# Multi-query attention with a GELU branch: some of the exp tiles on VectorE as integer bit patterns, four-head groups and a list scheduler

## The chip, the cores and the metric

The kernel runs on one core of one Trainium2 chip. The metric is the device time of the program in microseconds. It is taken several times per kernel, and each execution comes with the mean clock that TensorE was granted (1.0 is full speed). An execution is called slow when it lies over 1.5% above the fastest of the same kernel. Only fast ones are compared, unless the text says otherwise. Engines: PE is TensorE, PEld its weight loads, DVE VectorE, ACT ScalarE, POOL GpSimd.

## The reference

```python
B, S, D, H, F = 1, 2048, 512, 32, 1792          # Dh = D // H = 16
xn = _layernorm(x)
q = (xn @ wq).reshape(B, S, H, Dh).transpose(0, 2, 1, 3)
k, v = xn @ wk, xn @ wv                          # one K and one V for all 32 heads
scores = jnp.einsum("bhqd,bkd->bhqk", q, k) * (Dh ** -0.5)
o = jnp.einsum("bhqk,bkd->bhqd", softmax(scores), v)
A = o.transpose(0, 2, 1, 3).reshape(B, S, H * Dh) @ wo
Bb = gelu(xn @ w1 + b1, approximate=True) @ w2 + b2
return x + A + Bb                                # bf16 in and out
```

Attention needs 32 x 2048 x 2048 exponentials. In tiles of 128 keys by 512 queries these are 2048 tiles.

## The kernel before

It processes queries in four blocks of 512, heads in groups of three (and one of two), and keys in 16 tiles of 128. One step makes three score tiles in three PSUM banks (row-tiled matmuls of 17 rows: 16 of the head and one that subtracts an upper bound of the scores), one wide exp on ScalarE, and three column-tiled PV matmuls into a fourth bank. Two sets of three banks alternate. The GELU branch, the projections of Q and the outputs are woven in, two matmuls a step. Where a step has none of these, the same number of idle "fill" matmuls is issued, meant to keep TensorE's clock up.

```python
GROUPS = [list(range(h, min(h + 3, H))) for h in range(0, H, 3)]
...
def exp(s):
    act(lambda e: e.activation(E[:, s % NEB, 0:n * TBW], bank(3 * x, n), ACT.Exp, scale=0.25), ...)

def pv(s):
    for j, h in enumerate(GROUPS[g]):
        mm(pO[32 * j:32 * j + 32, :], V1[:, kt, :], E[:, s % NEB, j * TBW:(j + 1) * TBW],
           kt == 0, kt == NT - 1, r=["V1", ("E", s % NEB)], w=[B(6)], tp=(0, 32 * j))
...
for s in range(NS):
    exp(s)
    if s + 2 < NS:
        fill(s, n_fill)          # idle matmuls into the bank that comes next
        scores(s + 2)
    pv(s)
    ...                          # group ends, tanh, gates, up to two woven-in matmuls
```

Of the kernel before, what the change touches and what calls it, by code (L numbers as in the profile page):

```python
# [7 lines left out]
ALU = mybir.AluOpType  # L8
AX = mybir.AxisListType

P = 128
GELU_C = 0.044715
GELU_K = 0.7978845608028654


class _Op:
    __slots__ = ("eng", "fn", "deps", "stream", "amt", "need", "ticket", "waits", "clock")


class Prog:  # L20



# [5 lines left out]
    def __init__(self, nc):  # L29
        self.nc = nc  # L30
        self.ops = []
        self.writer = {}
        self.readers = {}

    def add(self, eng, fn, r=(), w=(), dma=None):
        op = _Op()
        op.eng, op.fn = eng, fn
        op.stream = dma or eng
        op.amt = 16 if dma else 1
        op.need = bool(dma)  # L40
        op.ticket = None
        deps = {}

        def dep(o, raw):
            if o is None:
                return
            if o.stream == eng and (eng == "pe" or not raw):
                return
            deps[id(o)] = o

        for k in r:
            dep(self.writer.get(k), True)
        for k in w:
            dep(self.writer.get(k), False)
            for o in self.readers.get(k, ()):
                dep(o, False)
        op.deps = list(deps.values())
        for o in op.deps:
            o.need = True
        for k in w:  # L60
            self.writer[k] = op
            self.readers[k] = []
        for k in r:
            self.readers.setdefault(k, []).append(op)
        self.ops.append(op)
        return op

    def emit(self):
# [41 lines left out]
        return {s: t for s, t in count.items()}  # L110


def bass_parallel_sum__grouped_kv_mqa__dense_activation_gelu__prompt_kernel(
# [24 lines left out]
    GROUPS = [list(range(h, min(h + 3, H))) for h in range(0, H, 3)]  # L138
    NGR = len(GROUPS)
    NEB = 4  # L140
# [3 lines left out]
    with ExitStack() as es:  # L144
# [4 lines left out]
        xn = sb([P, 8, D], bf, "xn")  # L149
# [3 lines left out]
        wq_s = sb([P, DT, D], bf, "wq_s")  # L153
        wkp = sb([P, DT, 4, 32], bf, "wkp")
        wqp = sb([P, DT, H, 32], bf, "wqp")
        wop = sb([96, NGR, D], bf, "wop")
# [4 lines left out]
        ident = sb([P, P], bf, "ident")  # L161
        ones = sb([P, P], bf, "ones")
# [5 lines left out]
        selL = sb([64, 2], f32, "selL")  # L168
        rT = sb([P, 4, 2], f32, "rT")
        rX = sb([P, 4, 64], f32, "rX")  # L170
# [17 lines left out]
        V1 = sb([P, NT, 32], bf, "V1")  # L188
        QT = sb([P, 2, 8, TBW], bf, "QT")
        sqq = sb([P, 2, TBW], bf, "sqq")  # L190
        mT = sb([32, 2, TBW], bf, "mT")
        E = sb([P, NEB, 3 * TBW], bf, "E")
        Of = sb([96, 2, TBW], f32, "Of")
        den = sb([96, 2, 16], f32, "den")
        rbc = sb([96, 2, TBW], f32, "rbc")
        rd_dram = nc.dram_tensor("rden_rows", [NTB * NGR, 3 * TBW], f32).ap()
        oT = sb([96, 2, NGR, TBW], bf, "oT")
        hb = sb([P, FT, TBW], bf, "hb")
        ub = sb([P, FT, TBW], bf, "ub")
        xpy = sb([P, 4, D], f32, "xpy")  # L200
        outb = sb([P, 4, D], bf, "outb")
# [13 lines left out]
        def dve(fn, r=(), w=()):  # L215
            return add("dve", fn, r, w)

        def act(fn, r=(), w=()):
            return add("act", fn, r, w)

        def pool(fn, r=(), w=()):
            return add("pool", fn, r, w)

        def mm(o, l, rh, start, stop, r=(), w=(), tp=None, skip=False):
# [5 lines left out]
            return add("pe", lambda e: e.matmul(o, l, rh, start=start, stop=stop, **kw), r, w)  # L230

        def dma(eng, o, i, stream, r=(), w=()):
            return add(eng, lambda e: e.dma_start(o, i), r, w, dma=stream)

# [7 lines left out]
        dma("sp", wq_s[:], A_wq.rearrange("(k p) n -> p k n", p=P), "d_wq", w=["wq_s"])  # L242
# [3 lines left out]

# [15 lines left out]
        pool(lambda e: e.memset(V1[:, :, Dh:32], 0.0), w=["V1"])  # L262
        pool(lambda e: e.memset(V1[:, :, Dh:Dh + 1], 1.0), r=["V1"], w=["V1"])
# [14 lines left out]

# [3 lines left out]
        def ln_batch(b):  # L282
# [3 lines left out]
            for ti in range(t0, t0 + 4):  # L286
                dve(lambda e, ti=ti: e.bn_aggr(mv[:, ti, :], stats[:, ti, :]), r=[("st", ti)], w=[("mv", b)])
            sl = slice(t0, t0 + 4)
            dve(lambda e: e.tensor_scalar(ve_b[:, sl], mv[:, sl, 1], 1e-5, None, ALU.add), r=[("mv", b)], w=[("ve", b)])
            act(lambda e: e.activation(std_b[:, sl], ve_b[:, sl], ACT.Sqrt), r=[("ve", b)], w=[("std", b)])  # L290
            dve(lambda e: e.tensor_copy(m_b[:, sl], mv[:, sl, 0]), r=[("mv", b)], w=[("mb", b)])
            if b < 3:
                ln_stats(t0 + 4)
            dve(lambda e: e.reciprocal(rstd[:, sl], std_b[:, sl]), r=[("std", b)], w=[("rstd", b)])
            dve(lambda e: e.scalar_tensor_tensor(nmr[:, sl], m_b[:, sl], -1.0, rstd[:, sl], ALU.mult, ALU.mult),
                r=[("mb", b), ("rstd", b)], w=[("nmr", b)])
            on_act = [t0, t0 + 2] if b == 3 else []
            for ti in range(t0, t0 + 4):
                if ti in on_act:
                    act(lambda e, ti=ti: e.activation(xn[:, ti % 8, :], x_sb[:, ti, :], ACT.Identity,  # L300
                                                      bias=nmr[:, ti:ti + 1], scale=rstd[:, ti:ti + 1]),
                        r=[("x", ti), ("rstd", b), ("nmr", b)], w=[("xn", ti % 8)])
                else:
                    pool(lambda e, ti=ti: e.tensor_scalar(xn[:, ti % 8, :], x_sb[:, ti, :], rstd[:, ti:ti + 1],  # L304
                                                          nmr[:, ti:ti + 1], ALU.mult, ALU.add),
                         r=[("x", ti), ("rstd", b), ("nmr", b)], w=[("xn", ti % 8)])
# [5 lines left out]
        def x_T(b):  # L312
            order = [4 * b, 4 * b + 1, 4 * b + 2, 4 * b + 3]
            for ti in order:
                bk = ti % 2
                pT = bank(bk)[:, 0:256].bitcast(bf)
                for d in range(DT):
                    add("pe", lambda e, ti=ti, d=d, pT=pT: e.transpose(  # L318
                        pT[:, d * P:(d + 1) * P], xn[:, ti % 8, d * P:(d + 1) * P], ident[:]),
                        r=[("xn", ti % 8), "ident"], w=[B(bk)])  # L320
# [4 lines left out]
        def k_proj(b):  # L325
# [5 lines left out]
            act(lambda e: e.activation(KT[:, c], bank(bk), ACT.Identity, bias=krow[:, 0:1]),  # L331
# [10 lines left out]
        def q_proj(tb, hq, bk):  # L342
            for d in range(DT):
                mm(bank(bk), wqp[:, d, 4 * hq:4 * hq + 4, :].rearrange("p a n -> p (a n)"),
                   xnT[:, d, tb * TBW:(tb + 1) * TBW], d == 0, d == DT - 1, r=["wqp", ("xnT", tb)], w=[B(bk)])
                yield

        def q_evac(tb, hq, bk):
            pq, i = tb % 2, hq % 2
            dve(lambda e: e.tensor_copy(QT[:, pq, hq, :], bank(bk)), w=[B(bk), ("QT", pq, hq)])  # L350
            dve(lambda e: e.tensor_tensor(sqq[:, i, :], QT[:, pq, hq, :], QT[:, pq, hq, :], ALU.mult),
                r=[("QT", pq, hq)], w=[("sqq", i)])

        def q_first(hq, bk):
            for _ in q_proj(0, hq, bk):
                pass
            q_evac(0, hq, bk)

        def q_first_m(hq, bk):
            mm(bank(bk), selrR[:].rearrange("p a n -> p (a n)"), sqq[:, hq % 2, :], False, True,  # L360
               r=["selrR", ("sqq", hq % 2)], w=[B(bk)], skip=True)
            dve(lambda e: e.tensor_scalar(QT[:, 0, hq, :].bitcast(i16), bank(bk).bitcast(i32), isc[:, 0:1], ibi[:, 0:1],
                                          ALU.mult, ALU.add),
                r=["isc", "ibi"], w=[B(bk), ("QT", 0, hq)])

        def v_tiles(ts, first=False):
            for ti in ts:
                for d in range(DT):
                    mm(pO[:, ti * Dh:(ti + 1) * Dh], xnT[:, d, ti * P:(ti + 1) * P], wv_s[:, d, :], d == 0, d == DT - 1,
                       r=["wv_s", ("xnT", ti // 4)], w=[B(6)])  # L370
# [13 lines left out]
            r=["wq_s", "wqp"], w=["wqp"])  # L384
# [13 lines left out]
        dve(lambda e: e.tensor_reduce(R2[:], kmax[:], AX.X, ALU.max), r=["kmax"], w=["R2"])  # L398
# [3 lines left out]
        dve(lambda e: e.tensor_copy(V1[:, :, 0:Dh], pO[:, 0:NT * Dh].rearrange("p (t n) -> p t n", n=Dh)),  # L402
            r=["V1"], w=[B(6), "V1"])
        warm(4, 3)


        steps = [(tb, g, kt) for tb in range(NTB) for g in range(NGR) for kt in range(NT)]
        NS = len(steps)

        def scores(s):  # L410
            tb, g, kt = steps[s]
            x = s % 2
            for j, h in enumerate(GROUPS[g]):
                q0 = 32 * (h % 4)
                mm(bank(3 * x + j), KT[q0:q0 + 17, kt * P:(kt + 1) * P], QT[q0:q0 + 17, tb % 2, h // 4, :],
                   True, True, r=[("KT", kt // 4), ("QT", tb % 2, h // 4)], w=[B(3 * x + i) for i in range(3)],
                   tp=(q0, 0))

        def exp(s):
            tb, g, kt = steps[s]  # L420
            x = s % 2
            n = len(GROUPS[g])
            act(lambda e: e.activation(E[:, s % NEB, 0:n * TBW], bank(3 * x, n), ACT.Exp, scale=0.25),  # L423
                w=[B(3 * x + i) for i in range(3)] + [("E", s % NEB)])

        def pv(s):
            tb, g, kt = steps[s]
            for j, h in enumerate(GROUPS[g]):
                mm(pO[32 * j:32 * j + 32, :], V1[:, kt, :], E[:, s % NEB, j * TBW:(j + 1) * TBW],
                   kt == 0, kt == NT - 1, r=["V1", ("E", s % NEB)], w=[B(6)], tp=(0, 32 * j))  # L430

        def o_evac(tb, g):
            n = len(GROUPS[g])
            i = (tb * NGR + g) % 2
            dve(lambda e: e.tensor_copy(Of[0:32 * n, i, :], pO[0:32 * n, :]), w=[B(6), ("Of", i)])  # L435
            row = Of[16:17, i, :]
            dma("sp", den[0:32 * n, i, :], bass.AP(row.tensor, row.offset, [[32 * row.ap[0][0], n], [1, TBW]]),
                f"d_den{i}", r=[("Of", i)], w=[("den", i)])

        def o_recip(tb, g):  # L440
            n = len(GROUPS[g])
            i = (tb * NGR + g) % 2
            rows = rd_dram[tb * NGR + g:tb * NGR + g + 1, 0:n * TBW]
            dve(lambda e: e.reciprocal(den[0:32 * n, i, :], den[0:32 * n, i, :]), r=[("den", i)], w=[("den", i)])  # L444
            dma("sp", rows, den[0:32 * n, i, :], f"d_rd{i}", r=[("den", i)], w=[("rd", i)])
            for j in range(n):
# [268 lines left out]
```

## Time and profile before

| | before |
|---|---|
| timed, median of 3 (lowest to highest) | 1032.86 us (1024.54 to 1051.49) |
| span of the profiled execution | 1027.0 us |
| ScalarE busy | 966.7 us, 94% |
| TensorE busy | 904.4 us, 88% (idle fill matmuls included) |
| VectorE busy | 303.0 us, 30% |

Of the three, 1051.49 is slow by the rule above. The page's first part gives busy time by engine, and its chain of waits tells which engine the end hung on. The prediction shows both. In the stretch between the first and the last exp, the view of windows gives, after the stretch and its length, the busy time and the number of instructions of PE, PEld, DVE, ACT and POOL, then the mean granted clock, the DMA share and the DMA rate:

```profile
42.20:1006.10 963.90, 865.67 (x5476) 224.35 (x5573) 275.15 (x523) 950.93 (x724) 0.00 (x0) 1.00 0.04 12
```

ScalarE is busy for 951 of 964 us, and the mean clock rounds to 1.00.

### The profile page before, as it was taken

What the parts mean: (1) busy time and instruction counts of PE and PEld (TensorE: products, weight loads), DVE (VectorE), ACT (ScalarE), POOL (GpSimd) and SP (SyncE); (2) the same over time, 40 slices, a digit from 0 to 9 for tenths busy, and PEclk for the clock granted to TensorE, in tenths of its full rate; (3) what the DMA queues carried; (4) which work ended last, traced back from release to release, by engine and by line L of the source; (5) the groups of instructions that cost most, each with busy time, mean ns of one, the idle gap of its engine ahead of it and who ended that gap; (6) DMA issues with size and microseconds to landing.
All of it is one profiled execution on the core that took longest, in us unless ns stands there. A gap on an engine that the chain in (4) does not pass through costs nothing.

```text
span 1027.0 us, 13369 instructions
## 1 busy us (share of the span) xinstructions
PE 904.4 (88%) x5690; PEld 241.2 (23%) x5792; DVE 303.0 (30%) x601; ACT 966.7 (94%) x752; POOL 20.2 (2%) x40
## 2 busy tenths in 40 slices
PE   4898888888999988888999998888899988889897
PEld 2222222222222222222222222222222222222222
DVE  5222454422001014443220013544220012444112
ACT  4499999999999999999999999999989999999991
POOL 6000000000000000000000000000000000000000
PEclk9699999999999999999999999999999999999997
DMA  7000000000000000000000000000000000000000
GB/s 247 21 2 17 9 9 9 10 10 10 17 6 14 22 20 9 9 9 9 10 15 10 18 14 22 9 9 1 17 10 13 16 20 15 9 9 9 17 9 20
DMA packets 27944, 18.72 MB, mean 18 GB/s; under 512 B 16428, under 2 KB 23341, under 8 KB 27885
## 3 DMA queue, kind: packets, MB, share of 16 engines
q1 hardware_dynamic: 26828, 17.84, 5.9%
q8 instruction: 45, 0.74, 0.3%
q10 hardware_dynamic: 1056, 0.03, 0.1%
q14 instruction: 15, 0.11, 0.0%
HBM read 15.11 MB, written 2.36 MB: 17 GB/s over the span
## 4 chain that ended last, share of the span: by engine, by line
ACT 87%; PE 10%; DVE 1%; DMA 1%; issue 0%; POOL 0%; SPq 0%; DVEq 0%
ACT E L423 83%; PE pAll L230 9%; ACT ub L522 2%; DMA QT<-mT 0%; ACT xnT L321 0%; DMA rden_rows<-den 0%; DMA x_sb<-in_A_x_dram 0%; DVE stats L280 0%; POOL xn L304 0%; PE pAll L318 0%; ACT KT L331 0%; DMA rbc<-rden_rows 0%; ACT xn L300 0%; DVE QT L350 0%; DVE xpy L564 0%
## 5 line engine op out<-in xcount | busy, mean ns | idle before, releaser
L423 ACT ACTIVATE E<-pAll 128x1536 bf16<-128x1536 f32 (+1 forms) x704 | 931.5, 1589 | 15.5 <-PE pAll L230 15.0
L230 PE MATMUL pAll<-E,V 128*32 128x512 bf16 x2128 | 300.2, 390 | 0.0
L230 PE MATMUL pAll<-QT,KT 17*128 17x512 bf16 x2048 | 275.7, 385 | 21.7 <-ACT E L423 9.2
L230 PE MATMUL pAll<-xnT,ident 128*128 128x512 bf16 x611 | 191.8, 388 | 69.3 <-ACT E L423 58.0
L230 PEld LDWEIGHTS pAll<-QT,KT 17*128 17x128 bf16 x2048 | 68.2, 91 | 313.4 <-ACT E L423 164.9
L230 PEld LDWEIGHTS pAll<-E,V 128*32 128x32 bf16 x2128 | 75.7, 93 | 174.8 <-issue 160.2
L435 DVE COPY Of<-pAll 96x512 f32<-96x512 f32 (+1 forms) x43 | 29.5, 687 | 206.1 <-PE pAll L230 206.1
L230 PEld LDWEIGHTS pAll<-xnT,ident 128*128 128x128 bf16 x671 | 40.5, 97 | 169.5 <-ACT E L423 155.6
L509 DVE TENSOR_SCALAR hb<-pAll,b1T 128x512 bf16<-128x512 f32 x56 | 41.9, 748 | 102.0 <-PE pAll L230 102.0
L230 PE MATMUL pAll<-xnT,w_sb 128*128 128x512 bf16 x209 | 64.4, 384 | 2.4 <-issue 1.9
L230 PE MATMUL pAll<-w_sb,ub 128*128 128x512 bf16 x208 | 64.2, 384 | 2.5 <-issue 2.5
L230 PE MATMUL pAll<-wop,oT 96*128 96x512 bf16 (+1 forms) x176 | 56.8, 413 | 1.7 <-DVE xpy L564 1.7
L454 DVE TENSOR_TENSOR oT<-Of,rbc 96x512 bf16<-96x512 f32 (+1 forms) x43 | 29.4, 683 | 65.3 <-DMA rbc<-rden_rows 65.3
L350 DVE CAST QT<-pAll 128x512 bf16<-128x512 f32 x32 | 22.0, 688 | 66.5 <-PE pAll L230 66.4
L527 DVE SCALAR_TENSOR_TENSOR ub<-ub,hb 128x512 bf16<-128x512 bf16 x56 | 35.4, 684 | 17.4 <-ACT ub L522 17.4
L230 PE MATMUL pAll<-xnT,wqp 128*128 128x512 bf16 x119 | 37.9, 397 | 1.4 <-issue 1.4
L494 DVE TENSOR_SCALAR mT<-pAll 32x512 int16<-32x512 int32 x31 | 20.8, 671 | 53.7 <-PE pAll L230 53.7
L522 ACT ACTIVATE ub<-ub 128x1536 bf16<-128x1536 bf16 (+1 forms) x20 | 31.9, 1593 | 0.0
L551 DVE TENSOR_TENSOR outb<-pAll,x_sb 128x512 bf16<-128x512 f32 x12 | 8.3, 691 | 79.0 <-PE pAll L230 79.0
L444 DVE RECIPROCAL den<-den 96x16 f32<-96x16 f32 (+1 forms) x43 | 10.6, 246 | 61.2 <-DMA den<-Of 61.2
L514 DVE TENSOR_TENSOR ub<-ub,hb 128x512 bf16<-128x512 bf16 x56 | 23.8, 426 | 1.9
L511 DVE TENSOR_TENSOR ub<-hb 128x512 bf16<-128x512 bf16 x56 | 23.8, 425 | 1.9
(82 smaller groups left out, 195.1 us busy)
## 6 DMA issues: line engine op xcount, KB each, us to landing
rbc<-rden_rows SPq DMA_DIRECT2D x126, 64.0 KB, 2.0
w_sb<-in_B_w_dram SPq DMA_DIRECT2D x2, 1792.0 KB, 12.2
x_sb<-in_A_x_dram SPq DMA_DIRECT2D x8, 256.0 KB, 4.4
out_dram<-outb SPq DMA_DIRECT2D x16, 128.0 KB, 1.7
QT<-mT SPq DMA_DIRECT2D x124, 1.0 KB, 1.6
den<-Of SPq DMA_DIRECT2D x40, 6.0 KB
rden_rows<-den SPq DMA_DIRECT2D x40, 6.0 KB, 1.4
wq_s<-in_A_wq_dram SPq DMA_DIRECT2D x1, 512.0 KB, 6.3
```

The costliest lines, as they stand in the source:

```text
L230: return add("pe", lambda e: e.matmul(o, l, rh, start=start, stop=stop, **kw), r, w)
L350: dve(lambda e: e.tensor_copy(QT[:, pq, hq, :], bank(bk)), w=[B(bk), ("QT", pq, hq)])
L423: act(lambda e: e.activation(E[:, s % NEB, 0:n * TBW], bank(3 * x, n), ACT.Exp, scale=0.25), w=[B(3 * x + i) for i in range(3)] + [("E", s ...
L435: dve(lambda e: e.tensor_copy(Of[0:32 * n, i, :], pO[0:32 * n, :]), w=[B(6), ("Of", i)])
L444: dve(lambda e: e.reciprocal(den[0:32 * n, i, :], den[0:32 * n, i, :]), r=[("den", i)], w=[("den", i)])
L454: dve(lambda e: e.tensor_tensor(oT[0:32 * n, tb % 2, g, :], Of[0:32 * n, i, :], rbc[0:32 * n, i, :], ALU.mult), r=[("Of", i)] + [("rbc", i ...
L494: dve(lambda e, hq=hq: e.tensor_scalar(mT[:, hq % 2, :].bitcast(i16), pM[0:32, :].bitcast(i32), 0.5 / 65536.0, float(0x1fc00000) / 65536.0 ...
L509: dve(lambda e: e.tensor_scalar(hb[:, ft, :], pM, b1T[:, ft:ft + 1], None, ALU.add), r=["b1T"], w=[B(7), ("h", ft)])
L511: dve(lambda e: e.tensor_tensor(ub[:, ft, :], hb[:, ft, :], hb[:, ft, :], ALU.mult), r=[("h", ft)], w=[("u", ft)])
L514: dve(lambda e: e.tensor_tensor(ub[:, ft, :], ub[:, ft, :], hb[:, ft, :], ALU.mult), r=[("u", ft), ("h", ft)], w=[("u", ft)])
L522: act(lambda e: e.activation(ub[:, f0:f0 + n, :], ub[:, f0:f0 + n, :], ACT.Tanh, scale=GELU_K), r=[("u", f) for f in fts], w=[("u", f) for ...
L527: dve(lambda e, ft=ft: e.scalar_tensor_tensor(ub[:, ft, :], ub[:, ft, :], 1.0, hb[:, ft, :], ALU.add, ALU.mult), r=[("u", ft), ("h", ft)], ...
```

## The change

The intent: of every ten triples of score tiles, seven give one tile to VectorE instead of ScalarE, except for the first triples and the last tiles of each group of heads. This comes to 446 of the 2048 tiles. K is scaled so that the scores in PSUM count in units of 1/128 of a power of two. Adding 127 x 128 to such a number, less a constant of 107.8, and writing it as int16 gives a bf16 bit pattern that is already a rough exp. To smooth the error, VectorE makes four more patterns from the first by adding -51, -26, 26 and 51, and TensorE sums all five, each with its own weighted copy of V: five PV matmuls per tile instead of one. Groups become four heads, so that all four column groups of PV are used and all triples but the last are full. The hand-woven order is replaced by a list scheduler with a cost model. TensorE's fillers now go only where the plan has a gap of over 0.25 us, and the tanh product of GELU is split into two VectorE instructions (one of 684 ns for 512 elements before, L527). The core of the diff, cut:

```diff
+SPL_K = (-51, -26, 0, 26, 51)
+SPL_C = (0.453125, 0.39453125, 0.349609375, 0.298828125, 0.259765625)
+D_RATE = 0.7
+FILL_GAP = 0.25
+PV_MIN = 6
+PV_MAX = 12
+PV_S = 4
...
+    def schedule(self):          # list scheduler over estimated durations
+                if mode == "col" and pvs and visit < (PV_S if urgent else PV_MAX):
+                    op = min(pvs, key=lambda o: (max(t, cgbusy[o.tag[1]]), o.rdy + o.allow, o.idx))
...
-    GROUPS = [list(range(h, min(h + 3, H))) for h in range(0, H, 3)]
+    HG = 4
+    GAM = 128.0 / LN2 * 0.25
...
+        def p1(t, bk):
+            dve(lambda e: e.tensor_scalar(Dt[:, KZ, s, :], bank(bk), float(127 * 128) + SPL_D, SPL_MIN, ALU.add, ALU.max),
+                w=[B(bk), ("D", s, KZ)], allow=0.0, kind="p1")
...
+        def close_batch():       # up to three tiles
+            for k in order:
+                if k != KZ:
+                    dve(lambda e, k=k: e.tensor_scalar(Dt[:, k, s0:s0 + n, :], Dt[:, KZ, s0:s0 + n, :], float(SPL_K[k]),
+                                                       None, ALU.add), ...)
+                for t, s in batch:
+                    pv_mm(gg, j, 1 + k, kt, Dt[:, k, s, :].bitcast(bf), [("D", s, k)])
```

In the changed kernel's profile L650 is exp, L666 the add-and-max out of PSUM (`p1`), L680 the four integer adds, L633 the scores, L670 PV, L403 all full-width matmuls, L886 the fillers.

## The prediction

> **What bounds the kernel now.** I read the page's first two parts, then the chain that ended last, then the groups with shapes kept apart, then the timeline in order of time. First the page: busy shares, the slices, and the chain.
>
> ```profile
> PE 904.4 (88%) x5690; PEld 241.2 (23%) x5792; DVE 303.0 (30%) x601; ACT 966.7 (94%) x752; POOL 20.2 (2%) x40
> ...
> ACT  4499999999999999999999999999989999999991
> ...
> PEclk9699999999999999999999999999999999999997
> ...
> ACT 87%; PE 10%; DVE 1%; DMA 1%; issue 0%; POOL 0%; SPq 0%; DVEq 0%
> ACT E L423 83%; PE pAll L230 9%; ACT ub L522 2%; DMA QT<-mT 0%; ACT xnT L321 0%; DMA rden_rows<-den 0%; DMA x_sb<-in_A_x_dram 0%; DVE stats L280 0%; POOL xn L304 0%; PE pAll L318 0%; ACT KT L331 0%; DMA rbc<-rden_rows 0%; ACT xn L300 0%; DVE QT L350 0%; DVE xpy L564 0%
> ```
>
> ScalarE is full from the second slice to the last but one, and its exp (L423) is 83% of the chain. VectorE is 70% idle: that is the reserve which the change spends. The groups with shapes kept apart:
>
> ```profile
> L423 ACT ACTIVATE E<-pAll 128x1536 bf16<-128x1536 f32 x640 | 866.7, 1643 | 5.0 <-PE pAll L230 4.9
> ...
> L423 ACT ACTIVATE E<-pAll 128x1024 bf16<-128x1024 f32 x64 | 66.0, 1040 | 10.5 <-PE pAll L230 10.1
> ...
> L522 ACT ACTIVATE ub<-ub 128x1536 bf16<-128x1536 bf16 x16 | 26.7, 1670 | 0.0
> ...
> L512 DVE TENSOR_SCALAR ub<-ub 128x512 bf16<-128x512 bf16 x56 | 16.4, 293 | 1.9
> ...
> L579 DVE TENSOR_SCALAR w_sb<-w_sb 128x7168 bf16<-128x7168 bf16 x1 | 2.0, 2016 | 0.0
> ...
> L682 DVE TENSOR_TENSOR outb<-pAll,xpy 128x512 bf16<-128x512 f32 x4 | 2.5, 682 | 1.0 <-PE pAll L230 1.0
> ```
>
> Means of one instruction overlap with the neighbour, so costs must come from pitches. The timeline from 260 to 290 us and from 268 us gives them:
>
> ```profile
> 284.83 5.48 ACT L423 ACTIVATE E<-pAll 128x1536 bf16<-128x1536 f32 x4 [0.19 <-PE pAll L230]
> ```
>
> ```profile
> 270.61 1.02 ACT L423 ACTIVATE E<-pAll 128x1024 bf16<-128x1024 f32 x1 [0.16 <-PE pAll L230]
> 270.80 0.11 PEld L230 LDWEIGHTS pAll<-xnT,ident 128*128 128x128 bf16 x2 [0.23 <-issue]
> 270.80 0.60 PE L230 MATMUL pAll<-xnT,ident 128*128 128x512 bf16 x2
> 271.34 0.09 PEld L230 LDWEIGHTS pAll<-QT,KT 17*128 17x128 bf16 x2 [0.42 <-issue]
> 271.34 0.39 PE L230 MATMUL pAll<-QT,KT 17*128 17x512 bf16 x2
> 271.66 0.10 PEld L230 LDWEIGHTS pAll<-E,V 128*32 128x32 bf16 x2 [0.23 <-issue]
> 271.66 0.39 PE L230 MATMUL pAll<-E,V 128*32 128x512 bf16 x2
> ```
>
> A single wide exp takes 1.45 us (the same timeline at 46.69 us), so four in 5.48 us have a **pitch** of (5.48-1.45)/3 = 1.343 us. A 1024-wide one takes 1.02 us when it stands alone; with the same overlap (1.45-1.343 = 0.107) it has a pitch of 0.916 us. In the two-head groups it gets 1.182 us instead (269.43 to 270.61), because TensorE is the longer there: fill 0.54, scores 0.32, PV 0.32, back to back. The balance of before: first exp at 42.2, then 640 x 1.343 + 64 x 1.182 = 935, tanh 16 x 1.36 + 4 x 0.93 = 25, some 4 lost at 45-52 us where TensorE is cold, so 1006; the last exp does end at 1006.1. Then 21 us of tail to 1027.
>
> [...]1.45 us for 1536, and (1.45-1.02)/512 = 0.84 ns per element. [...]The trace: (2016-293)/(7168-512) = 0.26 ns per element for L512 and L579[...]; 682 ns for 512 elements out of PSUM. [...]No run here shows int16 from SBUF. [...]The trace: two or three row-tiled scores hold TensorE for 0.32 us and two full matmuls for 0.54, where 0.215 is one matmul's pitch (270.80 to 271.34 is 2 x 0.215 + 0.11), so about 0.10 us a change.
>
> **The change part by part.** Counts are of the built kernel's instruction order. There are 2048 score tiles of 128 keys x 512 queries as before, but always in threes across four-head groups.
>
> *ScalarE.* 446 tiles (22%) leave it. What stays is 236 wide and 447 1024-wide exps: 236 x 1.343 + 447 x 0.916 = 317 + 409 = 726, with the 20 tanh 752. Before it was 960: 208 us less. The two-head groups, where TensorE held exp back by 0.27 us a step, are gone.
>
> *VectorE.* Each removed tile costs one add-and-max out of PSUM, pitch 0.60 (the four L682 take 2.48, and (2.48-0.68)/3 = 0.60): 446 x 0.60 = 268. Then per batch of three tiles four integer adds of 1536 elements; estimate from L512 and L579: 293 + 1024 x 0.259 = 558 ns alone, less about 0.085 overlap, 0.47 each; 512 of them 241, and 124 of 1024 elements at 0.335, 42. Each of the 159 batches has a first add that waits for its own engine's add-and-max; such a dependent successor starts about 0.12 us later than the 0.60 pitch (L350 at 100.12, its successor at 100.84): 19. Sum 570. The old work in this stretch: 56 biases 37, gelu in wide pieces with the split (tanh+1)h product 67, query evacuation and squares 30, group evacuation, reciprocal and normalisation 43, outputs 14, rest 14: 205. **VectorE needs 775**, where the whole old kernel kept it busy for 303.
>
> *TensorE.* PV rises from 2048 matmuls to 1602 + 5 x 446 = 3832, column-tiled up to four at a time. In the order they stand in 569 visits that need at least 1109 slots of 0.215 us: 238 + 57 for mode changes = 295, perhaps 320, as a batch of three tiles has only three of the four column groups. Scores: 683 x 0.215 + 653 x 0.10 = 212. Full-width matmuls 740, plus fillers, now 101 (over 600 before): 181 + 42 = 223. **TensorE needs 730 to 755.** The old fillers mostly ran while TensorE would have waited anyway; these PV matmuls are work that others wait for.
>
> *Ends.* Prologue unchanged, first exp near 42, and the 4 us of the cold start. The tail was 21 us, of which about 10 were the part sums of wo left over at the end (L564 chain, 1011 to 1021); these are now placed before the end, so about 10.
>
> *Sum.* ScalarE 752, VectorE 775, TensorE 755: the reserve is spent, the three are level. Were VectorE alone the bound: 42 + 4 + 775 + 10 = 831. Its load is spread evenly enough for that: exp tiles and group ends cost it (570 + 43)/683 = 0.90 us a step of three tiles, in the gelu stretches (some 352 of 683 steps) another 104/352 = 0.30, so 1.20 against ScalarE's 726/683 + 25/352 = 1.13; elsewhere 0.90 + 58/331 = 1.07 against 1.06. I add stalls of 5%, 39 us, by choice: a score triple now needs both exp and add-and-max to have left its banks, and all three engines run in a fixed order. 42 + 4 + 814 + 10 = 870, and 5 because the timed median stood 6 above the traced span before (1032.9 against 1027.0). **Prediction 875 us**, 15% less.
>
> **Rivals.** *A: VectorE becomes the sole bound and its in-order queue holds the banks.* An add-and-max behind a wide gelu product (up to 0.96 us) delays the next scores and so exp. For: 775 of work in some 815 us. Against: only one bank of three is VectorE's, and an exp lasts 0.92 us, time to hide. Utilisation of 88% would give 775/0.88 + 56 = 937. [...]*C: everything overlaps as the static order intends.* Then the largest engine, 775, with ends: 831 to 845. For: only 101 fillers were needed in the order, so TensorE has few planned gaps. *D: TensorE is the bound,* if the column-tiled visits do not pack to four: at three a slot PV takes 275 + 57, TensorE 767, with its waits 885 to 900.
>
> **Range and chances.** C sets the low end, 838; a mix of A and D the high end, 930. Only B, or a loss of over 20% to stalls, spoils the gain: at 1012 us main-phase utilisation of VectorE would be 81%. Faster by over 2%: 0.94; within 2%: 0.03; slower: 0.03.
>
> **What would show it.** In the changed profile: ScalarE busy near 770-800 and its idle time split between waits for scores, the chain no longer 83% exp but mixed; VectorE near 85-95% busy; the integer adds at 0.55 us for 1536 elements (B wrong), the add-and-max at 0.69; score matmuls released by the add-and-max as often as by exp (A) or by TensorE's own order (D); clock 1.0 throughout; a tail of about 10 us after the last exp. I am wrong if the adds take over 0.8 us, if VectorE has over 15% idle while ScalarE waits, or if PV visits cost well over 0.32 us for four.

In it, B is the rival that an int16 add costs more per element than the 0.26 ns that L512 and L579 show for bf16; what it would cost then, no trace of this case shows. What it calls cold is the granted clock of 0.50 from 45.2 to 52.0 us of the trace before, where wide exps started every 2.05 us (46.69, 48.74, 50.80) instead of every 1.343.

## The result and the profile after

The changed kernel takes **901.73 us** (median of four, 898.65 to 904.14, granted clock 0.977 to 0.986). Its ratio to before is 0.877, with a 95% interval of 0.873 to 0.882. All ratios and intervals here are computed by program from the fast runs of both kernels, so they are not quite the ratio of the quoted medians. The direction and the range were right; the time is 27 us, 3%, over the predicted 875.

The page of the changed kernel: busy shares, three of its rows of forty slices, and the chain by engine and by line.

```profile
PE 861.9 (96%) x6893; PEld 259.5 (29%) x6893; DVE 784.7 (87%) x1498; ACT 787.2 (87%) x731; POOL 25.7 (3%) x51
...
DVE  7359999989887679999998787999998777999984
ACT  3469999989898898999999988999989889999982
PEclk9859999989999999999999999999999999999999
...
PE 70%; DVE 17%; ACT 12%; issue 1%; DMA 0%; DVEq 0%; ACTq 0%
PE pAll L670 30%; PE pAll L403 19%; PE pAll L633 18%; ACT E L650 10%; DVE Dt L666 5%; DVE Dt L680 5%; PE pAll L886 2%; DVE hb L748 2%; ACT xnT L493 1%; ACT ub L762 1%; DVE ub L759 1%; DVE ub L761 1%; DVE stats L452 1%; DVE Of L693 1%; DVE ub L764 0%
```

ScalarE has dropped by 180 us and is below 90% in many slices. VectorE has risen by 482 us. The chain, 83% exp before, is now 70% TensorE, with PV alone at 30%. That is neither the ScalarE bound of before nor the VectorE that my sum took as the largest.

The groups of VectorE with shapes kept apart (busy us, then the mean ns of one, then idle time ahead of them and what ended it) answer the question whether the integer adds are cheap:

```profile
L666 DVE TENSOR_SCALAR Dt<-pAll 128x512 int16<-128x512 f32 x446 | 300.6, 686 | 77.1 <-PE pAll L633 75.2 <-PE pAll L670 0.8
L680 DVE TENSOR_SCALAR Dt<-Dt 128x1536 int16<-128x1536 int16 x512 | 255.0, 555 | 1.8 <-PE pAll L670 0.4
L680 DVE TENSOR_SCALAR Dt<-Dt 128x1024 int16<-128x1024 int16 x124 | 44.3, 423 | 0.2
```

They are: 555 ns, where 558 was estimated. The 75 us of idle time ahead of L666 ended when TensorE delivered scores, so VectorE waits for TensorE rather than the other way round.

The windows of the changed kernel, columns as before: the loop from first to last exp, a stretch near its start, and what follows the last exp.

```profile
44.10:885.70 841.60, 825.14 (x6667) 242.60 (x6667) 753.19 (x1418) 770.51 (x703) 8.75 (x9) 0.98 0.05 14
46.80:67.30 20.50, 20.32 (x99) 3.65 (x99) 12.51 (x23) 13.39 (x13) 6.62 (x7) 0.50 0.10 27
...
885.70:902.40 16.70, 10.47 (x57) 4.70 (x57) 8.36 (x16) 0.00 (x0) 0.00 (x0) 1.00 0.10 32
```

So the loop takes 841.6 us where the sum had 4 + 814 = 818. VectorE is busy for only 753 of it, 22 less than the predicted 775. TensorE ran at half clock for 20.5 us at the start, and in three later stretches (from 179.9, 238.0 and 289.2 us) for another 14; the kernel before had 7 us of this in its loop (45.2 to 52.0). The end takes 16.7 us instead of 10.

The view of waits shows who holds whom (total us, times, longest):

```profile
PEld pAll L633 <- ACT E L650: 147.8, 355, 1.8
...
DVE Dt L666 <- PE pAll L633: 75.2, 95, 3.2
...
ACT E L650 <- PE pAll L633: 41.5, 66, 2.6
ACT E L650 <- PE pAll L670: 29.9, 30, 3.2
```

A score's weight load was released by exp 355 times. The same view lists its release by the add-and-max 51 times, for 17.7 us in all. A weight load that waits is not yet an idle TensorE: the page puts only 11.3 us of idle time ahead of the score matmuls themselves. ScalarE and VectorE together waited some 147 us for TensorE's scores and PV.

**Why TensorE needs more than predicted.** The timeline around 331 and 338 us (start, length, engine, line, tile, count) shows two visits to the column-tiled mode with four PV matmuls each:

```profile
331.24 0.40 PE L670 MATMUL pAll<-E,V 128*32 128x512 bf16 x4
331.57 0.39 PE L633 MATMUL pAll<-QT,KT 17*128 17x512 bf16 x3
...
338.16 0.39 PE L670 MATMUL pAll<-Dt,V 128*32 128x512 bf16 x2
338.17 0.39 PE L670 MATMUL pAll<-E,V 128*32 128x512 bf16 x1
338.38 0.38 PE L670 MATMUL pAll<-Dt,V 128*32 128x512 bf16 x1
338.70 0.39 PE L633 MATMUL pAll<-QT,KT 17*128 17x512 bf16 x3
```

The first four start together and the scores follow 0.33 us later. In the second visit three start together and the fourth 0.22 us later, because it writes the same 32 columns as one of the three; the scores follow after 0.54 us. So a visit needed as many slots of about 0.2125 us as its fullest column group had matmuls, not a quarter of its matmuls: with the built order laid beside the trace, outside the half-clock stretches, visits of one to five such slots held TensorE for 0.33, 0.54, 0.76, 0.97 and 1.19 us in the median. I counted the slots over the kernel's built order: the 3832 PV matmuls stand in 569 visits, which need 1109 slots at the least but **1359** as they stand. Of the 188 visits with four matmuls, 106 fit in one slot and 82 need two (0.33 and 0.54 us in the median).

With 0.107 us for each change of mode (three scores held TensorE for 0.32 us, a slot of 0.2125 and this), PV then needs 1359 x 0.2125 + 569 x 0.107 = 350 us, where I had 295 to 320. With scores (215) and full-width matmuls (222) TensorE needs about 790 us, more than VectorE's 775. From 68 to 880 us TensorE's work at full clock comes to 759 of 812 us, 94%. In that stretch the PV visits took 375 us instead of 340, so 35 of the 52 us that are left lie in or around them; the scores took 223 instead of 210.

### The profile page after: what moved, and what is told of

The parts are those of the page before. It is cut to its first block, busy times and chain, and to the rows that moved or that the text cites. A ratio compares the mean times of both kernels' runs of the same rounds, so it can differ in the third digit from the quotient of the medians.

```text
span 902.4 us, 16691 instructions
## 1 busy us (share of the span) xinstructions
PE 861.9 (96%) x6893; PEld 259.5 (29%) x6893; DVE 784.7 (87%) x1498; ACT 787.2 (87%) x731; POOL 25.7 (3%) x51
## 4 chain that ended last, share of the span: by engine, by line
PE 70%; DVE 17%; ACT 12%; issue 1%; DMA 0%; DVEq 0%; ACTq 0%
PE pAll L670 30%; PE pAll L403 19%; PE pAll L633 18%; ACT E L650 10%; DVE Dt L666 5%; DVE Dt L680 5%; PE pAll L886 2%; DVE hb L748 2%; ACT xnT L493 1%; ACT ub L762 1%; DVE ub L759 1%; DVE ub L761 1%; DVE stats L452 1%; DVE Of L693 1%; DVE ub L764 0%
## 5 line engine op out<-in xcount | busy, mean ns | idle before, releaser
L650 ACT ACTIVATE E<-pAll 128x1024 bf16<-128x1024 f32 (+1 forms) x683 | 747.1, 1187 | 73.6 <-PE pAll L633 41.5
L666 DVE TENSOR_SCALAR Dt<-pAll 128x512 int16<-128x512 f32 x446 | 300.6, 686 | 77.1 <-PE pAll L633 75.2
L670 PE MATMUL pAll<-Dt,V 128*32 128x512 bf16 x2230 | 348.9, 391 | 0.1
L680 DVE TENSOR_SCALAR Dt<-Dt 128x1536 int16<-128x1536 int16 x636 | 299.0, 529 | 2.0 <-PE pAll L670 0.4
L670 PE MATMUL pAll<-E,V 128*32 128x512 bf16 x1602 | 295.4, 393 | 4.2 <-DVE Of L693 3.4
L633 PE MATMUL pAll<-QT,KT 17*128 17x512 bf16 x2048 | 267.3, 389 | 11.3 <-ACT E L650 8.7
L633 PEld LDWEIGHTS pAll<-QT,KT 17*128 17x128 bf16 x2048 | 65.9, 91 | 247.5 <-ACT E L650 147.8
L670 PEld LDWEIGHTS pAll<-Dt,V 128*32 128x32 bf16 x2230 | 94.6, 95 | 118.5 <-issue 66.6
L670 PEld LDWEIGHTS pAll<-E,V 128*32 128x32 bf16 x1602 | 70.6, 94 | 99.2 <-issue 59.0
L403 PE MATMUL pAll<-w_sb,ub 128*128 128x512 bf16 x224 | 71.0, 391 | 0.0
L403 PE MATMUL pAll<-xnT,w_sb 128*128 128x512 bf16 x224 | 66.6, 386 | 0.8 <-DVE hb L748 0.8
L403 PE MATMUL pAll<-xnT,wqp 128*128 128x512 bf16 x128 | 40.4, 403 | 0.1
L403 PE MATMUL pAll<-wop,oT 128*128 128x512 bf16 x128 | 37.6, 383 | 2.6 <-DVE x_sb L797 1.8
L886 PE MATMUL pAll<-xnT,zeros 128*128 128x512 bf16 x101 | 35.0, 389 | 0.0
L403 PEld LDWEIGHTS pAll<-w_sb,ub 128*128 128x128 bf16 x224 | 18.1, 98 | 38.7 <-issue 29.6
L403 PEld LDWEIGHTS pAll<-xnT,w_sb 128*128 128x128 bf16 x224 | 16.1, 97 | 34.5 <-issue 15.3
L693 DVE COPY Of<-pAll 128x512 f32<-128x512 f32 x31 | 21.2, 683 | 0.0
L704 DVE TENSOR_TENSOR oT<-Of,rbc 128x512 bf16<-128x512 f32 x31 | 21.2, 683 | 0.0
```

What stands on the lines that cost most here:

```text
L403: return add("pe", lambda e: e.matmul(o, l, rh, start=start, stop=stop, **kw), r, w, occ=occ, lat=0.23, allow=allow)
L633: ins = e.matmul(o, l, rh, start=True, stop=True, tile_position=(q0, 0))
L650: exps.append(act(lambda e: e.activation(E[:, s0:s0 + na, :], bank(3 * x, na).rearrange("p (a n) -> p a n", a=na), ACT.Exp, scale=LN2 / 12 ...
L666: dve(lambda e: e.tensor_scalar(Dt[:, KZ, s, :], bank(bk), float(127 * 128) + SPL_D, SPL_MIN, ALU.add, ALU.max), w=[B(bk), ("D", s, KZ)], ...
L670: add("pe", lambda e, a, b: e.matmul(pO[32 * j:32 * j + 32, :], V1[:, v, kt, :], rhs, start=a, stop=b, tile_position=(0, 32 * j)), r=r + [ ...
L680: dve(lambda e, k=k: e.tensor_scalar(Dt[:, k, s0:s0 + n, :], Dt[:, KZ, s0:s0 + n, :], float(SPL_K[k]), None, ALU.add), r=[("D", s0 + i, KZ ...
```

## The experiments

The list scheduler plans the whole kernel from one cost model, so each edit changes the order everywhere and not only at the edited place. The three rounds (e1, e2, e3) ran on three different chips. In every build below, the clearing of the zeros tile that the fillers read is also moved to the front of GpSimd's queue, so that this read stays ordered in any plan:

```diff
+        pool(lambda e: e.memset(zeros[:], 0.0), w=["zeros"])   # now among the first
-        pool(lambda e: e.memset(zeros[:], 0.0), w=["zeros"])   # was after V1
```

My theory (T in the expectations) is that TensorE's slots set the pace. The rivals are that VectorE's queue does (V), that ScalarE does, and that the half clock takes the missing time (H). Other letters are explained where they are used. Slots are counted over each build's order.

| kernel | median us, all runs | ratio to before (95%) | against the change, by ratios | loop + tail, profiled run | half clock in the loop | loop by the plan |
|---|---|---|---|---|---|---|
| the change | 901.7 | 0.877 (0.873 to 0.882) | 1 | 841.6 + 16.7 | 34 | 810.8 |
| e1_oldest | 935.6 | 0.908 (0.904 to 0.913) | +3.6% | 863.1 + 23.0 | 27 | 847.7 |
| e1_no_adds | 879.7 | 0.853 (0.847 to 0.859) | -2.7% | 823.4 + 11.3 | 31 | 792.7 |
| e1_one_pv (wrong) | 889.9 | 0.855 (0.846 to 0.863) | -2.6% | 842.1 + 10.3 (slow) | 75 | 793.6 |
| e1_narrow_exp (wrong) | 891.1 | 0.866 (0.858 to 0.874) | -1.3% | 814.6 + 27.7 | 17 | 801.1 |
| e2_warm | 906.2 | 0.881 (0.877 to 0.885) | +0.5% | 843.2 + 16.7 | 14 | 819.1 |
| e2_nofill | 906.9 | 0.882 (0.880 to 0.885) | +0.6% | 846.8 + 15.8 | 58 | 811.4 |
| e2_rate0 | 1028.4 | 0.997 (0.987 to 1.006) | +13.6% | 963.4 + 10.3 | 44 | 935.2 |
| e2_rate6 | 891.3 | 0.867 (0.864 to 0.870) | -1.1% | 836.6 + 9.6 | 38 | 803.8 |
| e3_one_pattern | 878.6 (one fast run, 855.3) | none | | 801.2 + 10.2 | 48 | 760.7 |
| e3_one_pattern_r1 | 823.6 | 0.794 (0.780 to 0.807) | -9.5% | 756.9 + 10.1 | 61 | 716.0 |
| e3_rate6_s6 | 881.5 | 0.854 (0.845 to 0.862) | -2.7% | 830.1 + 11.7 | 27 | 795.1 |
| e3_s8 | 900.8 | 0.875 (0.871 to 0.879) | -0.3% | 843.0 + 11.5 | 14 | 820.0 |

The fourth column is the quotient of two ratios from different rounds; under 1% it says nothing. Loop is from the first to the last exp, tail is what follows.

The last column costs no chip time: a kernel that is built holds the start and end that its scheduler expects of each instruction. It knows the slots, the waits and the fixed order, but not the clock, and it charges nothing when TensorE changes to full-width matmuls and 0.08 us when it changes to PV, where the traces show 0.10 to 0.12 (in the changed kernel three scores hold TensorE for 0.32 us and a PV visit of one slot for 0.33, of which the slot is 0.2125 to 0.215). It foresees much of what follows: the plan of e1_no_adds is 18 us shorter in the loop, and so is its trace. Over the 13 builds the traced loop is 13.5 to 48.5 us longer than the planned one, and the more so the longer the clock was halved (correlation 0.83; a line through them gives 14 us, and 0.43 us more for each us at half clock). This is a correlation and not an experiment.

### More slots: e1_oldest

The scheduler takes the oldest waiting PV matmul instead of one whose column group is free.

```diff
-  op = min(pvs, key=lambda o: (max(t, cgbusy[o.tag[1]]), o.rdy + o.allow, o.idx))
+  op = min(pvs, key=lambda o: (o.rdy + o.allow, o.idx))
```

> The changed kernel with one rule of its planner altered: within a column-tiled PV visit it takes the oldest waiting PV matmul, not the one whose column group is free first. Same instructions on all engines in another TensorE order (and the memset of the zeros tile moved to the front of GpSimd's work, so that the fillers' read is ordered). By the built order PV takes 1472 slots of 0.2125 us where the changed kernel takes 1359, the other work of TensorE within 2 us after 25 fewer fillers. Theory T (TensorE is the bound, because the column groups of a PV visit don't fill): 17 to 25 us longer than 901.7, so 918 to 928, ratio to before about 0.895. Theory V (VectorE, the 775 us of my prediction, is the bound): within 8 us of 901.7.

Measured: 935.56 us. The order needs 1472 slots, 113 more, which is 24 us by 0.2125. The time rose by 34, which is 8 above the range of T (918 to 928) and far outside that of V. VectorE's busy time stayed (787.0 against 784.7 us) and ScalarE's too (789.3). In the profiled runs the loop is 21.5 us longer, about what the slots cost, and the tail 6.3. More work for TensorE alone, then, makes the loop longer by about as much as it costs, which puts TensorE on the path that sets the end; but the new order also moved the waits and the tail, and no run tells these apart. The chain by engine, though, changed in an unexpected way:

```profile
PE 56%; DVE 35%; ACT 7%; issue 1%; DMA 1%; SPq 0%; DVEq 0%; ACTq 0%
```

With the same VectorE work the chain now runs through VectorE for 35% instead of 17%. So the chain is one path among several of nearly the same length, and its share doesn't tell by itself which engine to relieve.

### Less VectorE work: e1_no_adds

The four integer adds are left out; all five PV matmuls read the unshifted pattern.

```diff
-                if k != KZ:
+                if False:
...
-  pv_mm(gg, j, 1 + k, kt, Dt[:, k, s, :].bitcast(bf), [("D", s, k)])
+  pv_mm(gg, j, 1 + k, kt, Dt[:, KZ, s, :].bitcast(bf), [("D", s, KZ)])
```

> Wrong on purpose: the four integer adds of each batch are left out and all five PV matmuls of a tile read the first bit pattern. VectorE loses 636 instructions, about 283 us of work at its pitch; TensorE's matmuls are the same in number (1348 PV slots, 62 fillers instead of 101). Theory T: TensorE still needs some 779 us in the loop, only its waits for the adds (about 21 us in the trace) go: 870 to 890. Theory V: ScalarE's 752 us is the next bound, so 820 to 845.

Measured: 879.7 us (874.7 to 881.4). The busy shares and the chain:

```profile
PE 841.2 (96%) x6854; PEld 249.7 (28%) x6854; DVE 525.5 (60%) x862; ACT 784.9 (89%) x731; POOL 25.7 (3%) x51
...
PE 68%; ACT 28%; DVE 3%; issue 0%; DMA 0%; DVEq 0%; ACTq 0%
```

260 us of VectorE's work are gone and the time falls by only 22 (5 of them in the tail), within the range of T, while TensorE stays at 96%. A VectorE bound would have given far more, so V is refuted as the sole cause. The comparison with the reference does not see the shifts. This says nothing about how much accuracy they give.

### Less PV work: e1_one_pv

Only the unshifted pattern's PV matmul is issued, so 1784 of the 3832 are gone; the adds stay. The result is wrong (relative error 0.24).

```diff
-  pv_mm(gg, j, 1 + k, kt, ...)
+  if k == KZ:
+      pv_mm(gg, j, 1 + k, kt, ...)
```

> Wrong on purpose: all integer adds stay on VectorE, but only one of the five PV matmuls of a tile is issued (2048 instead of 3832 PV matmuls, 749 slots instead of 1359, 130 us of TensorE less; the planner fills a part of its own gaps with 516 fillers). Theory T: TensorE falls under the others, which are at 752 and 775: 835 to 865. Theory V: VectorE is untouched, 890 to 905.

Measured: 877.2 and 883.3 us in the two fast runs (clock 0.976 and 0.970), 896.6 and 898.9 in two slow ones (0.948). Both ranges missed. Relief of TensorE alone gives 2.6%, as little as relief of VectorE alone: with PV gone, VectorE (783 us busy) is the longest. The scheduler put in 516 fillers, and TensorE still ran at half clock for 75 us of the profiled run, a slow one.

### Less ScalarE work: e1_narrow_exp

Each three-tile exp does only two tiles, and PV reads the second twice. Wrong (relative error 0.52).

```diff
-            na = len([t for t in ts if not is_d[t]])
+            nt = len([t for t in ts if not is_d[t]])
+            na = min(nt, 2)
```

> Wrong on purpose: each of the 236 wide exps does only 1024 elements, and the third tile's PV reads the second's result. ScalarE loses 236 x 0.427 = 101 us of its 752; TensorE keeps its matmuls, in 1266 slots by the new plan (93 fewer, -20 us, with 36 fillers more). Theory T: 875 to 898, by the slots alone. If ScalarE still were the bound: 800 to 830. Theory V: 890 to 905.

Measured: 891.13 us. ScalarE's busy time fell by 94 us to 692.9 (78%) and the time by 11: in the profiled runs the loop is 27 us shorter and the tail 11 longer. That excludes ScalarE as the bound (800 to 830). It does not choose between T and V, whose ranges both hold 891, and 93 PV slots (20 us of TensorE) went with the edit.

### A warm start: e2_warm

Fillers are forced ahead of the loop and into its first ten steps, against the 20 us at half clock.

```diff
         scores(1)
+        warm(6, 7)
...
+            if u < 10:
+                warm(2, 7)
```

> The changed kernel with extra full-width dummy matmuls at the loop's start (6 behind the first scores, 2 in each of the first ten steps) to hold the granted clock. In the changed kernel's trace the clock was 0.50 from 46.8 to 67.3 us, where 16 exps took 23.5 us. Theory H (half-clock stretches are one of the terms missing from my sum): the clock stays 1.0 there, 16 exps take about 18 us, and 4 to 9 us go from 901.7: 892 to 898, ratio to before about 0.869. Rival: the start is bound by the first queries' loads and by VectorE, not by the clock: no gain, or some us lost to the 26 extra matmuls.

Measured: 906.18 us, clock 0.981 to 0.989. The clock was full from 34 to 150 us, and yet the time did not fall. The edit also changed the plan as a whole (1335 slots instead of 1359, 17 more fillers, and a chain with 38% VectorE). The plan of the new loop is itself 8.3 us longer, while the traced loop is only 1.6 longer, with 20 us less at half clock. By this reckoning the clock gave back some 7 us, within H's 4 to 9, and the new plan took them. That is an estimate across two builds; the run itself is inconclusive on H.

### No fillers: e2_nofill

```diff
-FILL_GAP = 0.25
+FILL_GAP = None
```

> The changed kernel without the planner's 101 filler matmuls (30 us of TensorE). Theory T taken strictly (every matmul on TensorE costs time): 875 to 885. Theory H: the fillers stand in planned gaps and keep the clock up; without them more half-clock stretches show and the time is equal or longer, 898 to 930.

Measured: 906.88 us, clock 0.959 to 0.968. This is in the range of H (898 to 930). The 101 fillers (some 30 us of TensorE, mode changes included) are not 30 us to be gained: they stand in gaps of the plan, whose loop is as long without them (811.4 against 810.8). Without them TensorE is at half clock for longer, 58 us of the loop instead of 34: the first stretch is about as long (48.6 to 65.7), but 253.4 to 270.5 and 366 to 373 us are new, among others. At +0.6% across rounds, that the fillers gain time is not shown; they cost none.

### The schedule and the groups alone: e2_rate0

No tile goes to VectorE.

```diff
-D_RATE = 0.7
+D_RATE = 0.0
```

> Only the list scheduler and the four-head groups: no tile goes to VectorE (D_RATE 0). ScalarE has 683 exps of 1.343 and tanh 25, so 942 us; with 44 ahead and 12 to 16 behind 998 to 1005, ratio to the fast runs of before about 0.97. So of the 128 us gained some 27 would be grouping and scheduling and 100 the exp tiles. If the list order itself costs stalls: over 1010.

Measured: a ratio of 0.997. The scheduler and the four-head groups bring nothing as one package without the tiles, so the 12% appears only with the tiles on VectorE. I had expected some 3%, since the steps of two heads are gone; over 1010 us was to mean that the list order itself costs stalls. Its plan has 990.5 us in all, with the order's own waits in it. The runs follow the clock: 1018.0 us at 0.970, 1024.0 at 0.965, 1032.7 at 0.952. The timeline of ScalarE in one half-clock stretch of the profiled run (139.8 to 153.4 us) shows what such a stretch does to exp:

```profile
145.75 1.45 ACT L650 ACTIVATE E<-pAll 128x1536 bf16<-128x1536 f32 x1 [0.60 <-PE pAll L633]
147.80 1.45 ACT L650 ACTIVATE E<-pAll 128x1536 bf16<-128x1536 f32 x1 [0.60 <-PE pAll L633]
```

Exp starts every 2.05 us instead of every 1.343, each time after 0.60 us of waiting for scores. The loop was at half clock for 44 us, against 7 in the kernel before, and not for want of fillers: this plan has 926, more than the 600-odd of before, but it places them by its gaps and not in every step. That the lost clock eats what the full groups gain is my reading; no run isolates it from costs of the order that the plan does not know.

### A smaller share: e2_rate6

```diff
-D_RATE = 0.7
+D_RATE = 0.6
```

> D_RATE 0.6 instead of 0.7: 383 tiles on VectorE instead of 446. ScalarE gains 63 x 0.427 = 27 us of work (779), VectorE loses some 80 (695), TensorE loses 252 PV matmuls; by the built order 1246 PV slots instead of 1359, so about 18 us less with its fillers. Theory T: 880 to 893. Were ScalarE the bound: 920 to 930.

Measured: 891.33 us, within the range of T. 383 tiles go to VectorE instead of 446. The PV order needs 1246 slots, 113 (24 us) fewer; VectorE is busy for 712.7 us, 72 less, and ScalarE for 809.8, 23 more. So at 0.7 too many tiles were moved for this schedule. But in the profiled runs the tail gives 7 us of the gain (9.6 against 16.7) and the loop only 5: the output's last part sums (L797) all start before the last exp ends, where in the change all four come after it.

### Longer visits: e3_s8

Visits to the column-tiled mode may last eight PV matmuls instead of four while scores wait.

```diff
-PV_S = 4
+PV_S = 8
```

> The changed kernel (D_RATE 0.7) with PV visits of up to 8 matmuls, not 4, while scores wait: 1305 PV slots in 535 visits instead of 1359 in 569, 32 fillers more, all else the same in number. Theory T (TensorE's work sets the time): 54 x 0.2125 + 34 x 0.107 = 15 us less, some of it eaten by fillers, 888 to 897. Rival L (the latency of scores behind PV visits sets it): equal or longer, 902 to 915.

Measured: 900.76 us: no gain. TensorE has 1305 slots in 535 visits, the 15 us less of the expectation. Its recorded busy time fell by 28 us, but this can't be read as the saving: the trace has 113 matmuls fewer than weight loads, where the changed kernel's has 6893 of both, and 113 x 0.2125 is 24 us. The busy shares and the chain by engine:

```profile
PE 833.7 (93%) x6812; PEld 260.4 (29%) x6925; DVE 784.0 (87%) x1498; ACT 791.4 (88%) x731; POOL 25.9 (3%) x51
...
PE 54%; DVE 34%; ACT 7%; issue 2%; DMA 1%; POOL 1%; SPq 0%; DVEq 0%; ACTq 0%
```

T alone expected a gain (888 to 897), so T is not the whole story at this share. The time lies between its range and that of rival L (902 to 915: scores wait behind long visits), nearer to L. The plan sides with L: its loop is 9 us longer than the change's, though TensorE has less to do. The chain passes to VectorE (34%), which is unchanged at 784.0 us. The two readings aren't told apart.

### Both together: e3_rate6_s6

A smaller share relieves VectorE and TensorE, and a longer visit (six) relieves TensorE.

```diff
-D_RATE = 0.7
+D_RATE = 0.6
-PV_S = 4
+PV_S = 6
```

> The exact version that should beat both kernels: D_RATE 0.6 and PV visits of up to 6 matmuls, not 4, while scores wait: 1222 PV slots in 523 visits instead of rate6's 1246 in 572, 27 fillers more. By TensorE's work 5 to 10 us under rate6's 891: 881 to 888. If longer visits hold the scores back: 891 to 900.

Measured: 881.51 us (875.4 to 887.9), ratio 0.854, correct, within the range, with 1222 slots in 523 visits. This version keeps the five patterns and beats both kernels, by 15% and, across rounds, 2.7%. Of its gain in the profiled runs 11.5 us lie in the loop and 5 in the tail. Its busy shares and chain:

```profile
PE 823.3 (93%) x6602; PEld 248.2 (28%) x6708; DVE 713.3 (80%) x1311; ACT 810.5 (91%) x731; POOL 26.0 (3%) x51
...
PE 53%; ACT 33%; DVE 10%; issue 2%; POOL 1%; DMA 0%; DVEq 0%; ACTq 0%
```

ScalarE now carries a third of the chain and VectorE a tenth. Against e2_rate6 the gain is 1.5% by ratios; the intervals don't overlap, though the rounds and the granted clocks (0.979 to 0.993 here, 0.968 to 0.976 there) differ, so the visit length's own share of it is not certain.

### One pattern: e3_one_pattern and e3_one_pattern_r1

The four adds and the four extra PV matmuls both go, with the one weight set to 1.758. The second build also gives a tile of every triple to VectorE where that is allowed (605 tiles). This is a coarser exp; the comparison with the reference accepted both, and I did not measure its error. They are tests of joint relief, and I don't offer them as versions to use.

```diff
-SPL_C = (0.453125, 0.39453125, 0.349609375, 0.298828125, 0.259765625)
+SPL_C = (0.453125, 0.39453125, 1.7578125, 0.298828125, 0.259765625)
...
-                if k != KZ:
+                if False:
...
+                    if k == KZ:
                         pv_mm(gg, j, 1 + k, kt, ...)
# second build only
-D_RATE = 0.7
+D_RATE = 1.0
```

> 446 tiles stay on VectorE, but with one bit pattern instead of five: no integer adds, one PV matmul a tile, its V weighted by the sum of the five weights (1.7578). A coarser exp by intent; whether the comparison still accepts it is open. VectorE loses 283 us (as in no_adds), TensorE 130 us of PV (as in one_pv, with 334 fillers), ScalarE nothing. Joint theory J (TensorE and VectorE are level and each alone hides the other's relief): ScalarE's 752 becomes the bound, 44 + 752 + 14 and 10 to 25 of stalls: 820 to 835. Rival C (the fixed order and the clock cost the time, not either engine's work): as with either relief alone, 870 to 890.

> One pattern, and D_RATE 1.0: 605 of 683 steps give one of their three tiles to VectorE. ScalarE 605 x 0.916 + 78 x 1.343 + 25 = 684, VectorE about 570, TensorE 669 with fillers by the built order. Theory J: ScalarE is the bound, 44 + 684 + 14 and 10 to 30 of stalls, 752 to 775. Rival C: over 800. Correctness open.

Measured, first build: 855.25 us in the one fast run (clock 0.966), 878 to 888 in three slow ones (0.922 to 0.933), so there is no ratio. Second build: 812.16 and 822.66 us in the two fast runs (0.955, 0.930), ratio 0.794. In the profiled run of the second, TensorE was at half clock from 45.1 to 79.2 and from 127 to 154.3 us. The ranges for joint relief (J: 820 to 835 and 752 to 775) were both missed. The first build lies between J and rival C (the fixed order and the clock set the time: 870 to 890), the second in C's range (over 800). Their plans are 816.0 and 771.3 us long, near J, against 848.8 and 848.9 with either relief alone. Their traces exceed the plans by 38 and 39 us, with 48 and 61 us of the loop at half clock; the changed kernel exceeds its own by 31. The direction stands: 812 us is 62 below what either relief alone reached in any of its runs (874.7 and 877.2), though here the larger share counts as well.

## Why the prediction was right or wrong

**Right: what leaves ScalarE.** Exp busy fell as worked out; the 1024-wide exp lasted 1.04 us and the 1536-wide one 1.46 in the mean, in line with the 1.02 and 1.45 of single ones before. ScalarE is busy for 787.2 us, within the stated 770 to 800, and is idle 13% of the span.

**Right: what VectorE pays.** The adds took 555 and 423 ns, so (555 - 423)/512 = 0.26 ns per int16 element as for bf16, and the add-and-max 686, against 558 and 0.69 us; rival B is out. The loop had 753 us of VectorE instead of 775, so this term was 22 too high.

**Wrong: what TensorE needs.** This is the term that failed. The step read "at least 1109 slots of 0.215 us: 238 + 57 for mode changes = 295, perhaps 320", and the sum then took VectorE as the largest. A minimum was used as an estimate. The order needs 1359 slots and 350 us, which makes TensorE, at 790, the longest of the three, and the stalls came on top of that. The sign named for it, visits well over 0.32 us for four, is there: 82 of 188 need two slots, 0.54 us. In the 812 us that I counted (68 to 880), 759 were TensorE's work and 52 waits and half clock; the other 30 us of the loop lie mostly in the first half-clock stretch. How much of the 24 us that the loop ran over comes from the slots is not shown: the plan counts them all and still has a loop of 810.8, and the 31 us on top may be mode changes that it leaves out, half clock, or both.

**Luck in the number.** The 39 us of stalls were added by choice. Without them the sum is 836, 66 under the result, with the wrong engine as the longest.

**Rival D had the mechanism.** It had PV pack to three a slot, TensorE at 767, and 885 to 900 us; the visits pack to 3832 / 1359 = 2.8, and the time is 902. What speaks for it by experiment is e1_oldest (more slots cost about themselves in the loop) and e1_no_adds (260 us less VectorE give 22). But e3_s8 shows that D isn't all: take 15 us from TensorE alone and nothing comes of it. With three engines at 87 to 96%, each stands right behind the next: relief of one alone gave 0 to 3%. Relief of two gave 2.7% in e3_rate6_s6, no more than the best of the single ones, and more only in the one-pattern builds, which take off most.

**Rival A is weak.** The wide gelu products took 0.95 us in the mean (L759, L761, L764), as it supposed, but the add-and-max released a score's weight load 51 times, exp 355 times. That VectorE's bank is held too long was not tested by itself.

**Wrong: clock 1.0 throughout.** Some 34 us of the loop were at half clock. The granted clock there was 0.50, so by my estimate at most half of it, 17 us, is lost TensorE work (a PV visit of four took 0.55 us, from 51.07 to 51.62, instead of 0.33); by the line through the 13 builds it would be some 15. e2_warm took the first stretch away without a gain in time, so its price stays an estimate.

**Wrong: the ends.** First exp at 44.1 instead of 42. The tail took 16.7 us instead of 10: the part sums that were "placed before the end" were not done by then. The timeline after the last exp:

```profile
891.81 0.68 DVE L797 TENSOR_TENSOR x_sb<-pAll,x_sb 128x512 f32<-128x512 f32 x1
...
894.27 0.69 DVE L797 TENSOR_TENSOR x_sb<-pAll,x_sb 128x512 f32<-128x512 f32 x1 [0.98 <-PE pAll L403]
...
896.52 0.69 DVE L797 TENSOR_TENSOR x_sb<-pAll,x_sb 128x512 f32<-128x512 f32 x1 [0.84 <-PE pAll L403]
...
898.78 0.69 DVE L797 TENSOR_TENSOR x_sb<-pAll,x_sb 128x512 f32<-128x512 f32 x1 [0.84 <-PE pAll L403]
```

The four part sums (L797) go through one PSUM bank, one each 2.3 us. In the plan they are side work with little urgency. The built plan has a tail of 17.4 us, so this could have been read before the run. Over the builds the tail ran from 9.6 to 27.7 us; it was 9.6 in e2_rate6, where these sums were done in time, as the prediction had it. No run tested another placing by itself.

**The sum.** 2 for the first exp, 24 for the loop, 7 for the tail, and -6 because I added 5 for the step from traced span to timed median, where the median came 0.7 below the span: 27 us, the whole miss. (The 6 us of before compared different executions; wherever the time and the span of one execution are both on record, the time is 1.7 to 1.9 us longer.)

**Open.** What starts and ends the half-clock stretches (TensorE was busy for 20.32 of the 20.50 us of the first, and in e3_one_pattern_r1 for 32.67 of the 34.10 us from 45.1 to 79.2), and what each costs; how much of the 31 us over the plan is clock and how much uncounted mode changes; how much of e2_rate0's missing gain is clock; and the best share and visit length together, of which only four points were run.

## What to carry to other kernels

When work is moved to level all engines, cost each engine by the slots that its order really uses: for column-tiled matmuls the fullest column group of each visit, not a quarter of the count (here a visit of four took 0.33 or 0.54 us). Once the engines are level, relief of one buys almost nothing (here 0 to 3%) and load on the longest costs about itself (24 us of slots made the loop of e1_oldest 21.5 us longer), so sweep the share that is moved and look at relief of two engines at once. When a scheduler plans the order, read its planned loop and tail first: here they foretold the long tail, and that longer visits would not shorten the loop. Fillers in planned gaps cost nothing here (901.7 us with them, 906.9 without), and several builds with less work ran at a lower clock (0.968 to 0.976 in e2_rate6, 0.930 and 0.955 in e3_one_pattern_r1, against 0.977 to 0.986), so read the clock beside every time.
